# Scores of 256 instead of 512 keys a matmul, another order of the gelu's operations and a shorter warm-up in a two-layer decode kernel

## The chip, the cores and the metric

The kernel runs on one core of a Trainium2 chip. The metric is the device time of one execution in microseconds; what is compared is the median of several executions. A profiled execution also has a span, from the first to the last instruction in its trace, and the mean clock that TensorE (PE) was granted, as a share of full speed. In the profile PE is TensorE's matmuls, PEld its weight loads, DVE VectorE, ACT ScalarE, POOL GpSimd, and SP the engine whose queue issues all the transfers.

## The reference

One token (a row of 640 numbers) goes through two identical layers, each an attention over a cache and a mixer with a small MLP. Both layers use the same weights and the same caches. Cut to what is computed:

```python
def attention(x, k_cache, v_cache, wq, wo):        # 32 heads of 192, the last 4096 cached positions
    q = (x @ wq) per head
    p = softmax(q . k * 192 ** -0.5)
    return (p . v) for all heads, joined, @ wo

def mixer(x, w1, w2, w3, w4):
    ...                                            # the part with w1 and w2 only shifts along the sequence
    h2 = gelu(layernorm(x1) @ w3) @ w4             # 1536 units
    return x1 + h2

x = x + attention(layernorm(x)); x = x + mixer(layernorm(x))     # layer 1
x = x + attention(layernorm(x)); x = x + mixer(layernorm(x))     # layer 2
```

With a sequence of one, the groups that are shifted by one or two places are all zero, so the kernel needs w3 and w4 alone.

## The kernel before

A layer has 32 heads in 8 groups of 4 (`GROUPS`, reversed in layer 1, which the code calls layer 0). A head's keys and its values are one block each of 128 x 6144 bf16 (1536 KB), loaded from HBM into one of 11 cells (`take`, `give`, a first-in first-out list). All transfers stand in one fixed list, `stream`, and are issued from SP in its order: the query weights, then keys and values alternating (the next group's keys beside this group's values), the output weights of each group, and at a layer's end w3 and w4. A load is issued when its cell's last reader is done. The engines run their instructions in the order in which the code emits them (`manual_schedule`).

Seven turned key blocks (heads 0 to 6, `NKEEP`) are kept from layer 1 for layer 2 in cells of their own, so towards the end of layer 1 fewer cells are left for the stream. The other heads are turned into one shared cell, `area`.

For each head: `transpose_quart` (L351 to L373) turns a quarter of the key block with a DVE transpose (L370), four for a block. `scores` (L414) multiplies with the head's query columns (`Qblk`, 128 x 16 weights) into PSUM, and the 16 columns of the four heads of a group add into the same rows. `next_scores` (L438) decides on the shape. With `n == 4`, each of four quarters of the keys has its own rows (0, 32, 64 and 96) and a matmul has 256 keys; with `n == 2`, two halves of the keys have two row bands, and a matmul has 512 keys. A head has 24 matmuls in the first form and 12 in the second. `wide` in `attention` puts the first four groups of layer 1 and the third to fifth of layer 2 in the second form.

In the first form the scores of the first two quarters (`S(h, 0)`) stand ahead of those of the other two (`S(h, 1)`), so they can run while DVE turns the second half; in the second form each pair of matmuls needs quarters of both halves of the block, and all scores come at `half == 1`.

`softmax_steps` turns a group's scores into probabilities: maximum over the keys (L457, DVE), two small transposing products (L462, L479, PE), the exponential (L485, ACT), a transpose (L492, DVE), the rearranging products (L503, PE). `pv` multiplies with the values (L549, PE; 16 matmuls a head) and ends with a DVE transpose of the result (L556), which `o_fold` (L562, PE) adds up. `out_proj` (L571) multiplies with the output weights.

The loop of a group emits, for each head: the value product of this group's head, then turning and scoring of a head of the next group, then `o_fold`. Where two neighbouring groups have different forms, the first head's scores of the next group come only after `spread_max`.

`mixer` multiplies with w3 (L835) in two halves of the units, applies the gelu to each half (L840 to L854; squares and exponential on ACT, the rest on DVE), and multiplies with w4 (L867). In layer 2 both weights are loaded in pieces, and part of them is still there from layer 1.

At the start `WARM` matmuls of 32 x 32 (L309) run on PE while the query weights are on their way.

Of the kernel before, what the change touches and what calls it, by code (L numbers as in the profile page):

```python
# [36 lines left out]
def kernel(  # L37
# [40 lines left out]
    WARM = 125  # L78
# [273 lines left out]
    area = [None]  # L352

    def transpose_quart(layer, h, q):

        if layer == 1 and h < NKEEP:
            return kept[h]
# [3 lines left out]
        if layer == 0 and h < NKEEP:  # L361
            if q == 0:
                kept[h] = take(("T", h))
            T = kept[h]
        else:
            if area[0] is None:
                area[0] = take(("area", layer))
            T = area[0]
        Tu = T[:, q * QUART:(q + 1) * QUART].bitcast(U32).rearrange("p (y j b) -> p j y b", y=NY, j=NJ4)
# [45 lines left out]

    def scores(h, T, parts, ST, hq):

        ng = NGK // ST.n
        Q = Qblk[:, h // QH % 2, hq * QHEAD:(hq + 1) * QHEAD].rearrange("p (f x) -> p f x", x=QW)
        T5 = T[:].rearrange("p (g f i t) -> p g f i t", f=NFB, g=NGK, i=P)  # L420
        for f in range(NFB):
            for t in range(2):
                n = 2 * f + t
                for i in parts:
                    r = ST.rows.start + 32 * i
                    nc.tensor.matmul(  # L426
                        ST.ps[r:r + QW, :].rearrange("p (g i) -> p g i", g=ng), lhsT=Q[:, n, :],
                        rhs=T5[:, i * ng:(i + 1) * ng, f, :, t],
                        start=(hq == 0 and n == 0), stop=(hq == QH - 1 and n == NCOL - 1))

# [7 lines left out]
    def next_scores(n):  # L438
        turn[0] += 1
        i = turn[0] % 2  # L440
        if n == NT:
            return SimpleNamespace(n=n, rows=slice(0, P), ps=ST_both[:, i * SW:(i + 1) * SW])
        return SimpleNamespace(n=n, rows=slice(i * P // 2, (i + 1) * P // 2), ps=ST_both)
# [5 lines left out]
    def softmax_steps(n, ST, sc):  # L449
        held = {}  # L450
        R, np_ = ST.rows, ST.n
        NR, W_ = R.stop - R.start, P * NGK // np_
        ST_ps = ST.ps[R, :]

        def part_max():
            pm = big.tile([P, 1], F32, name="pm")
            nc.vector.tensor_reduce(out=pm[R, :], in_=ST_ps, op=ALU.max, axis=AX.X)  # L457
            held["pm"] = pm

        def turn_max():  # L460
            pmT_ps = psm.tile([1, NR], F32, tag="psm")
            nc.tensor.transpose(pmT_ps[0:1, :], held["pm"][R, 0:1], ident[R, R])  # L462
            held["pmT"] = pmT_ps

        def full_max():
            ngm = big.tile([1, 2 * QH], F32, name="ngm")
            nc.vector.tensor_reduce(out=ngm[:], in_=held["pmT"][0:1, :].rearrange("o (q x m) -> o x q m", q=np_, m=NM),
                                    op=ALU.max, axis=AX.XY, negate=True)

            wide = o_bytes[0:1, W_:W_ + 2 * NR].bitcast(F32)  # L470
            nc.vector.tensor_scalar(  # L471
                out=wide.rearrange("o (q x m) -> o q x m", q=np_, m=NM),
                in0=ngm[:].unsqueeze(1).unsqueeze(3).broadcast_to([1, np_, 2 * QH, NM]),
# [3 lines left out]
        def spread_max():  # L477
            nb_ps = psm.tile([P, 1], F32, tag="psm")
            nc.tensor.matmul(nb_ps[R, :], lhsT=held["w"],  # L479
                             rhs=ones[0:1, 0:1], start=True, stop=True)  # L480
            nb_sb = big.tile([P, 1], F32, name="nb_sb")
            nc.scalar.copy(nb_sb[R, :], nb_ps[R, :])  # L482
            Pr = o_bytes[R, 0:W_]
            lpart = big.tile([P, 1], F32, name="lpart")
            nc.scalar.activation(out=Pr, in_=ST_ps, func=ACTF.Exp,  # L485
                                 bias=nb_sb[R, 0:1], scale=sc[R, 0:1], accum_out=lpart[R, 0:1])
            held["Pr"], held["l"] = Pr, lpart

        def turn_p():

            for i in reversed(range(0, W_, SW)):
                nc.vector.transpose(o_bytes[R, SW + i:2 * SW + i], o_bytes[R, i:SW + i])  # L492
            lh = big.tile([P, QH], F32, name="lh")
            nc.vector.tensor_scalar(out=lh[R, :], in0=hm[R, :], scalar1=held["l"][R, 0:1], scalar2=None, op0=ALU.mult)
            held["lh"] = lh

        def swap():
            ng = NGK // np_
            PT_ps = psm.tile([P, n, NJ4, NGK], F32, tag="psm")
            src = o_bytes[R, SW:SW + W_].rearrange("p (g j i) -> p i j g", g=ng, j=NJ4)  # L500
            for m in range(NM):
                for q in range(np_):
                    nc.tensor.matmul(PT_ps[32 * m:32 * (m + 1), :, :, ng * q:ng * (q + 1)],  # L503
                                     lhsT=Eq[R, R.start // 32 + q, :], rhs=src[:, m:QW:NM], start=True, stop=True)
# [417 lines left out]
```

## Time and profile before

| | |
|---|---|
| three runs | 536.26, 543.6, 535.41 us; median 536.26 |
| profiled execution | 536.26 us, span 534.5, mean granted PE clock 0.659 |
| busy in the span | PE 321.0 us (60%), PEld 177.2 (33%), DVE 287.4 (54%), ACT 42.4 (8%), POOL 2.7 (1%) |
| moved from HBM | 216.47 MB, 405 GB/s over the span |
| scores (L426) | 336 matmuls of 512 keys, 864 of 256 |
| key transposes (L370) | about 0.94 us a quarter, 3.5 to 3.7 us a block |

How to read the lines that follow. A line of the windows gives a stretch in us, its length, the busy time and the number of instructions of PE, PEld, DVE, ACT and POOL, the granted PE clock, the share of the 16 DMA engines that was busy, and GB/s. A line of the waits gives the engine and line that waited, what it waited for, the total in us, how often, and the longest. A line of the timeline gives start and duration in us, engine, line, operation, tile written <- tiles read, shapes and the number of instructions that it merges, and in brackets how long the engine had been idle and what ended it. A DMA line ends with the us from issue to landing. SPq stands for instructions of SP's queue.

### The profile page before, as it was taken

To read this page: it belongs to the slowest core of one execution; us is meant where nothing else is said; L and a number is where in the kernel's file an instruction comes from. 1 tells how busy PE (TensorE), PEld (TensorE's weight loads), DVE (VectorE), ACT (ScalarE), POOL (GpSimd) and SP (SyncE) were. 2 spreads that over 40 slices of the span, in tenths; PEclk is the share of its full clock that TensorE was granted. 3 is DMA by queue.
4 is the path that set the end of the run, shared out by engine and by line. 5 is a ranking of instruction groups with operands and counts; after the bars stand their busy time and mean duration, and the time that the engine had idled before them with its cause. 6 is when DMAs were issued, how large, how long until landed. Compare 5 with 4: busy or idle time off the path is not lost. (4 is left out here: it accounts for less than half of the span.)

```text
span 534.5 us, 9507 instructions
## 1 busy us (share of the span) xinstructions
PE 321.0 (60%) x4125; PEld 177.2 (33%) x4125; DVE 287.4 (54%) x561; ACT 42.4 (8%) x157; POOL 2.7 (1%) x12
## 2 busy tenths in 40 slices
PE   3155474755646666667755865656565655667766
PEld 3011231313224343334433632323222243434435
DVE  2055646455555576656723355555547476666732
ACT  1000000101001010101011111000010000101012
POOL 2000000000000000000000000000000000000000
PEclk9996667556675767655665677665666557676665
DMA  8999999999999999999999999999999999999992
GB/s 342 429 425 427 421 427 427 425 427 423 424 427 390 425 423 408 344 397 380 388 418 405 377 420 427 425 425 424 427 423 426 424 419 423 424 424 426 419 403 109
DMA packets 23949, 217.08 MB, mean 406 GB/s; under 512 B 2532, under 2 KB 3044, under 8 KB 8420
## 3 DMA queue, kind: packets, MB, share of 16 engines
q1 hardware_dynamic: 23908, 216.48, 97.7%
q8 instruction: 32, 0.52, 0.4%
q14 instruction: 9, 0.07, 0.0%
HBM read 216.47 MB, written 0.00 MB: 405 GB/s over the span
## 5 line engine op out<-in xcount | busy, mean ns | idle before, releaser
L426 PEld LDWEIGHTS <-Qblk 128*16 128x16 bf16 x1200 | 66.7, 111 | 195.5 <-issue 179.1
L556 DVE STREAM_TRANSPOSE o_sb<-O_ps 128x384 f32<-128x384 f32 x64 | 37.2, 582 | 138.7 <-PE O_ps L549 138.7
L426 PE MATMUL ST_ps<-cell_336,Qblk 128*16 128x256 bf16 (+1 forms) x408 | 72.9, 485 | 55.3 <-DVE cell_336 L370 52.5
L426 PE MATMUL ST_ps<-cell_3261,Qblk 128*16 128x256 bf16 (+1 forms) x456 | 71.2, 454 | 45.3 <-DVE cell_3261 L370 39.9
L549 PEld LDWEIGHTS <-PT 128*2 128x2 bf16 x1024 | 45.6, 101 | 26.4 <-issue 17.4
L563 ACT ACTIVATE oT<-oT_ps,rl 32x6 bf16<-32x6 f32 x64 | 16.5, 258 | 293.2 <-PE oT_ps L562 236.4
L492 DVE STREAM_TRANSPOSE o_sb<-o_sb 64x256 bf16<-64x256 bf16 (+1 forms) x23 | 10.2, 442 | 40.1 <-ACT o_sb L485 27.8
L562 PE MATMUL oT_ps<-o_sb,Lq 128*32 128x6 f32 x256 | 21.8, 194 | 15.1 <-DVE o_sb L556 14.5
L562 PEld LDWEIGHTS oT_ps<-o_sb,Lq 128*32 128x32 f32 x256 | 20.4, 142 | 31.2 <-issue 27.1
L387 PE MATMUL qT_ps<-xc,wq_sb 128*128 128x1 bf16 x480 | 15.8, 165 | 14.9 <-DMA wq_sb<-in_A_wq_dram 14.0
L387 PEld LDWEIGHTS <-wq_sb 128*128 128x128 bf16 x480 | 14.7, 104 | 18.3 <-DMA wq_sb<-in_A_wq_dram 15.1
L462 PE MATMUL pmT_ps<-ident,pm 128*1 128x128 f32 (+1 forms) x16 | 4.4, 273 | 19.0 <-DVE pm L457 19.0
L401 PE MATMUL Qrep_ps<-Xq,Lb 128*128 128x24 bf16 (+1 forms) x18 | 3.3, 181 | 18.9 <-DVE Xq L394 18.6
L394 DVE TENSOR_TENSOR Xq<-qT_ps,maskq 128x24 bf16<-128x24 f32 (+1 forms) x18 | 2.8, 154 | 20.5 <-PE qT_ps L387 20.5
L508 PE MATMUL l_ps<-lh,ones 128*128 128x4 f32 (+1 forms) x32 | 9.2, 356 | 5.1 <-ACT PT L506 5.1
L479 PE MATMUL nb_ps<-ones,o_sb 1*128 1x1 f32 (+1 forms) x32 | 7.2, 292 | 7.5 <-DVE o_sb L471 7.5
L503 PEld LDWEIGHTS <-Eq 128*32 128x32 bf16 (+1 forms) x200 | 4.1, 111 | 21.0 <-issue 10.6
L479 PEld LDWEIGHTS nb_ps<-ones,o_sb 1*128 1x128 f32 (+1 forms) x32 | 6.0, 241 | 14.7 <-issue 12.0
L508 PEld LDWEIGHTS l_ps<-lh,ones 128*128 128x128 f32 (+1 forms) x32 | 7.8, 301 | 8.4 <-ACT PT L506 8.1
L485 ACT ACTIVATE o_sb<-ST_ps,nb_sb,sc 128x256 bf16<-128x256 f32 (+1 forms) x16 | 10.5, 656 | 0.5
L482 ACT COPY nb_sb<-nb_ps 128x1 f32<-128x1 f32 (+1 forms) x16 | 2.5, 157 | 94.1 <-PE nb_ps L479 94.1
L503 PE MATMUL PT_ps<-o_sb,Eq 128*32 128x32 bf16 (+1 forms) x200 | 7.0, 251 | 4.9 <-DVE o_sb L492 4.6
(291 smaller groups left out, 475.6 us busy)
## 6 DMA issues: line engine op xcount, KB each, us to landing
wq_sb<-in_A_wq_dram SPq DMA_DIRECT2D x5, 1536.0 KB, 14.3
cell_334<-in_A_k_cache_dram SPq DMA_DIRECT2D x1, 1536.0 KB
cell_356<-in_A_k_cache_dram SPq DMA_DIRECT2D x1, 1536.0 KB, 26.6
cell_381<-in_A_k_cache_dram SPq DMA_DIRECT2D x1, 1536.0 KB, 27.2
cell_399<-in_A_k_cache_dram SPq DMA_DIRECT2D x1, 1536.0 KB
cell_453<-in_A_k_cache_dram SPq DMA_DIRECT2D x1, 1536.0 KB, 29.5
cell_519<-in_A_v_cache_dram SPq DMA_DIRECT2D x1, 1536.0 KB, 29.5
cell_521<-in_A_k_cache_dram SPq DMA_DIRECT2D x1, 1536.0 KB, 29.5
```

The lines of the kernel that those rows point to most:

```text
L387: nc.tensor.matmul(qT_ps[:, tl:tl + 1], lhsT=wq_sb[:, kc, t * P:(t + 1) * P], rhs=xc[:, kc:kc + 1], start=(kc == 0), stop=(kc == ND - 1))
L426: nc.tensor.matmul(ST.ps[r:r + QW, :].rearrange("p (g i) -> p g i", g=ng), lhsT=Q[:, n, :], rhs=T5[:, i * ng:(i + 1) * ng, f, :, t], start ...
L462: nc.tensor.transpose(pmT_ps[0:1, :], held["pm"][R, 0:1], ident[R, R])
L479: nc.tensor.matmul(nb_ps[R, :], lhsT=held["w"], rhs=ones[0:1, 0:1], start=True, stop=True)
L485: nc.scalar.activation(out=Pr, in_=ST_ps, func=ACTF.Exp, bias=nb_sb[R, 0:1], scale=sc[R, 0:1], accum_out=lpart[R, 0:1])
L492: nc.vector.transpose(o_bytes[R, SW + i:2 * SW + i], o_bytes[R, i:SW + i])
L503: nc.tensor.matmul(PT_ps[32 * m:32 * (m + 1), :, :, ng * q:ng * (q + 1)], lhsT=Eq[R, R.start // 32 + q, :], rhs=src[:, m:QW:NM], start=Tru ...
L508: nc.tensor.matmul(l_ps[:], lhsT=ones[R, :], rhs=held["lh"][R, :], start=True, stop=True)
L549: nc.tensor.matmul(O_ps[r:r + 2, :], lhsT=PT[:, hq, 2 * i:2 * i + 2], rhs=v_pair(V, h, 2 * i * Dh, 2 * Dh), start=(i < 4), stop=(i >= NB - 4))
L556: nc.vector.transpose(o_sb[:], O_ps.rearrange("p (e a c) -> p e c a", e=2, c=NA))
L562: nc.tensor.matmul(oT_ps[r, :], lhsT=Lq[:], rhs=o_sb[:, e, :, e], start=(e == 0), stop=(e == 1))
L563: nc.scalar.activation(oT[r, :], oT_ps[r, :], ACTF.Copy, scale=rl[r, 0:1])
```

## The change

Four edits at once. The form with 512 keys a matmul goes, with all that chose between the two (`wide`, `parts`, `n`, `rows`); every group scores 256 keys a matmul. The shared cell of turned keys is handed out by quarters, in the order of their turning; the cells, the loads and DVE's order of transposes stay as they are. The gelu of a half, `h * r / (1 + e)`, was computed as the reciprocal of `(1 + e) * (1 / (h * r))` and becomes `(h * r)` times the reciprocal of `(1 + e)`. And the warm-up has 29 matmuls instead of 125.

```diff
-    WARM = 125
+    WARM = 29
...
-    def scores(h, T, parts, ST, hq):
-
-        ng = NGK // ST.n
+    def scores(h, Ts, q0, ST_ps, hq):
+
+        ng = NGK // NT
...
-                for i in parts:
-                    r = ST.rows.start + 32 * i
+                for i, T4 in enumerate(views):
+                    r = 32 * (q0 + i)
                     nc.tensor.matmul(
-                        ST.ps[r:r + QW, :].rearrange("p (g i) -> p g i", g=ng), lhsT=Q[:, n, :],
-                        rhs=T5[:, i * ng:(i + 1) * ng, f, :, t],
+                        ST_ps[r:r + QW, :].rearrange("p (g i) -> p g i", g=ng), lhsT=Q[:, n, :],
+                        rhs=T4[:, :, f, :, t],
                         start=(hq == 0 and n == 0), stop=(hq == QH - 1 and n == NCOL - 1))
...
-    def next_scores(n):
+    def next_scores():
         turn[0] += 1
         i = turn[0] % 2
-        if n == NT:
-            return SimpleNamespace(n=n, rows=slice(0, P), ps=ST_both[:, i * SW:(i + 1) * SW])
-        return SimpleNamespace(n=n, rows=slice(i * P // 2, (i + 1) * P // 2), ps=ST_both)
+        return ST_both[:, i * SW:(i + 1) * SW]
...
-        def S(h, half, ST, hq):
-            if ST.n == NT and (layer == 0 or h >= NKEEP):
-                parts = 2 * half, 2 * half + 1
-            elif half == 1:
-                parts = range(ST.n)
-            else:
+        def S(h, half, ST_ps, hq):
+            if layer == 1 and h < NKEEP:
+                if half == 1:
+                    scores(h, [Th.pop((h, q)) for q in range(NT)], 0, ST_ps, hq)
+                    give(("T", h))
                 return
-            scores(h, Th[h], parts, ST, hq)
...
+            scores(h, [Th.pop((h, q)) for q in (2 * half, 2 * half + 1)], 2 * half, ST_ps, hq)
...
-        wide = range(2, 5) if layer == 1 else range(4)
-        parts = [NT // 2 if gi in wide else NT for gi in range(len(groups))]
...
                     T(h0, 0)
                     part_max()
                     T(h0, 1)
-                    if ST.n == ST_n.n:
-                        S(h0, 0, ST_n, 0)
+                    S(h0, 0, ST_n, 0)
                     turn_max()
                     full_max()
-                    if ST.n == ST_n.n:
-                        S(h0, 1, ST_n, 0)
+                    S(h0, 1, ST_n, 0)
                     spread_max()
-                    if ST.n != ST_n.n:
-                        S(h0, 0, ST_n, 0)
-                        S(h0, 1, ST_n, 0)
...
             nc.scalar.activation(ge[:], gu[:], ACTF.Exp, scale=rg[:, 0:1])
-
-            rh = sm.tile([P, HF], F32, name="rh")
-            nc.vector.tensor_scalar(out=rh[:], in0=hp, scalar1=rr[:, 0:1], scalar2=None, op0=ALU.mult)
-            nc.vector.reciprocal(rh[:], rh[:])
-            nc.vector.scalar_tensor_tensor(out=gu[:], in0=ge[:], scalar=1.0, in1=rh[:],
-                                           op0=ALU.add, op1=ALU.mult)
-            with nc.allow_low_precision(reason="the matmul's operand, bf16 as in the reference"):
-                nc.vector.reciprocal(hT[:, half * HF:(half + 1) * HF], gu[:])
+            nc.vector.tensor_scalar(out=gu[:], in0=ge[:], scalar1=1.0, scalar2=None, op0=ALU.add)
+            nc.vector.reciprocal(gu[:], gu[:])
+            nc.vector.scalar_tensor_tensor(out=hT[:, half * HF:(half + 1) * HF], in0=hp, scalar=rr[:, 0:1], in1=gu[:],
+                                           op0=ALU.mult, op1=ALU.mult)
```

## The prediction, made before the result was known

> **What bounds the kernel now.** I read the page's totals first, then the stages by windows, the waits, one loop of each kind, and the end.
>
> ```profile
> span 534.5 us, 9507 instructions
> q1 hardware_dynamic: 23908, 216.48, 97.7%
> ```
>
> The queue is busy for 97.7% of the span, so at first sight the transfers bound the kernel and PE and DVE (60% and 54%) do not. The stages, with the rate in the last column, say where that fails:
>
> ```profile
> 10.00:160.00 150.00, 76.49 (x689) 32.56 (x689) 74.59 (x122) 7.41 (x26) 0.00 (x0) 0.71 1.01 425
> ...
> 160.00:170.00 10.00, 6.44 (x118) 4.50 (x119) 6.92 (x18) 1.29 (x4) 0.00 (x0) 0.50 0.96 380
> ...
> 200.00:270.00 70.00, 47.76 (x614) 28.59 (x602) 45.13 (x74) 5.21 (x20) 0.00 (x0) 0.63 0.98 384
> ...
> 290.00:310.00 20.00, 15.86 (x392) 12.51 (x391) 7.78 (x40) 3.02 (x15) 0.00 (x0) 0.67 0.99 383
> ```
>
> 425 GB/s is what the queue gives when it is full. From 160 to 170, 200 to 270 and 290 to 310 us it gives about 10% less: there are too few free cells, so loads are issued late. Who holds the cells? The two longest waits of DVE, and of PE, between 40 and 270 us (total, times, longest):
>
> ```profile
> DVE o_sb L556 <- PE O_ps L549: 63.5, 27, 4.3
> DVE o_sb L492 <- ACT o_sb L485: 12.8, 4, 3.8
> ...
> PE ST_ps L426 <- DVE cell_336 L370: 44.5, 35, 2.6
> PE Qrep_ps L401 <- DVE Xq L394: 11.6, 6, 3.2
> ```
>
> Neither engine waits for a transfer in that stretch. PE waits for DVE's key transposes, and DVE for PE's value products, which stand behind the scores: a ring, PE to DVE to PE, sets the pace, and the loads run ahead of it. How far ahead, for one key block in layer 1:
>
> ```profile
> L370 DVE STREAM_TRANSPOSE cell_336<-cell_1230 x4: 928/936/951, 157.2 to 160.4; 128x768 uint32<-128x768 uint32 x4
> L131 SPq DMA_DIRECT2D cell_1230<-in_A_k_cache_dram x1: 327/327/327, 127.3 to 127.3; - x1
> DMA to landing us min/median/max: 10.5/10.5/10.5
> ```
>
> It landed at 127.3 + 10.5 = 137.8 us and was first read at 157.2, 19.4 us later. The same view gives 9.5 us for the last key block of layer 2 (issued 475.3, landed after 17.4, read at 502.2). So the ring is late, and the transfers suffer only through the cells that it holds.
>
> **The change part by part.**
>
> *Scores.* Seven of the sixteen groups go from 512 to 256 keys a matmul: 28 heads, each with 24 matmuls instead of 12. What a group of four heads takes, by windows from the first value product of one group to that of the next, 512 keys first (the first, second and fourth lines), 256 keys in the others:
>
> ```profile
> 69.40:103.20 33.80, 20.15 (x204) 9.12 (x202) 18.59 (x33) 2.32 (x8) 0.00 (x0) 0.65 1.01 424
> 103.20:137.40 34.20, 20.35 (x204) 9.10 (x202) 19.00 (x33) 2.32 (x8) 0.00 (x0) 0.60 1.01 425
> 170.00:199.25 29.25, 18.84 (x262) 11.43 (x260) 17.95 (x32) 2.11 (x8) 0.00 (x0) 0.68 1.01 426
> 372.60:406.80 34.20, 20.70 (x204) 9.17 (x202) 18.56 (x33) 2.32 (x8) 0.00 (x0) 0.60 1.01 425
> 439.70:469.00 29.30, 18.87 (x262) 11.49 (x260) 17.98 (x31) 2.11 (x8) 0.00 (x0) 0.67 1.01 424
> ```
>
> The loads of a group are eight blocks of 1536 KB and one of 960 KB: 8 x 3.70 + 2.31 = 31.9 us at 425 GB/s. With 512 keys the ring (34.2) is slower than the transfers and falls behind by some 2 us a group; with 256 keys (29.3) it is faster and catches up 2.6 us. The reason is in one head of each kind:
>
> ```profile
> 76.48 2.72 PE L426 MATMUL ST_ps<-cell_336,Qblk 128*16 128x512 bf16 x11 [1.13 <-DVE cell_336 L370]
> ...
> 183.82 1.44 PE L426 MATMUL ST_ps<-cell_336,Qblk 128*16 128x256 bf16 x11 [0.58 <-DVE cell_336 L370]
> ```
>
> With 512 keys eleven of twelve matmuls stand behind the last transpose; with 256 keys half of them are done under the transposes. Of PE's work 2.72 - 1.44 = 1.3 us a head leaves the ring; the vector maximum, the exponential and the probability transposes of a group also shrink (0.67 to 0.40, 0.77 to 0.56, 0.91 to 0.45 us by the groups by line).
>
> What the ring gains: in layer 1 three loops (33.8 + 34.2 + 32.6 - 3 x 29.25 = 12.9 us), and the first group, whose keys are turned and scored from 27.4 to 53.3 us although the fourth block lands by 27.4 + 3 x 3.7 = 38.5: with 3.6 us of transposes and 1.5 of scores behind it, 43.6, so 9.7 us. Together 22.6 us. In layer 2 three loops, 34.6 + 34.2 + 32.9 - 3 x 29.3 = 13.8 us. This can't all be kept: the transfers take over as the bound. What is left is what they lose now.
>
> Term A, loads issued late in layer 1: 10 x (425 - 380) / 425 = 1.06 us and 70 x (425 - 384) / 425 = 6.75 us, together 7.8. A floor of 0 (the cells are short because seven turned key blocks are kept, whatever the pace) and a ceiling of 7.8; I take 7.8, since the ring comes at least 11 us (three transfers) earlier to each release between 200 and 250 us, while loads there are issued only two transfers ahead (8 to 10 us to landing). From the last value block of layer 1 (issued 275.2, landed 286.9, waited for by PE until 287.0) the serial part, with the dip at 290 to 310, follows as it is.
>
> Term B, the end. The last matmul weights:
>
> ```profile
> 511.29 2.22 SPq L176 DMA_DIRECT2D cell_5312<-in_B_w_dram  x2
> 526.78 0.40 PEld L835 LDWEIGHTS <-cell_5312 128*128 128x128 bf16 x12
> ...
> cell_5312<-in_B_w_dram SPq DMA_DIRECT2D x2, 768.0 KB, 10.7
> ```
>
> The second piece of w3 is issued at about 513.1 and lands 10.7 us later, 523.8. Behind it stand half of its 48 matmuls for the first half of the units, about 0.7 us, so 524.5 where the trace has 528.1: 3.6 us. The last piece of w4 lands at 517.5 + 9.9 = 527.4, with a few matmuls and the 2.9 us from 531.6 to the end behind it: 530.6 at the earliest, a gain of 3.9. The smaller counts: 3.6. The ring has to be 3.6 of 9.5 us earlier for it, and layer 2 gives it 13.8.
>
> *gelu.* Per half 5 DVE operations become 4, but two of the five (0.22 and 0.19 us) lie under the 0.30 us exponential, and behind it now stand three (add, reciprocal, product) instead of two. One step of 0.19 us more for each half: +0.4 us at the end; the same in layer 1 is covered by PE's 1.3 us wait there for w4. Bounds: -0.4 (two operations fewer, if DVE's queue counted) and +0.8. I take +0.4, by the exponential's row.
>
> *Warm-up.* 96 matmuls fewer of 125 (3.5 us, from 3.85 us). PE waits 14.0 us for the query weights behind them (the group of L387), so 0; if that cover were gone, at most 3.5 x 96/125 = 2.7 us won.
>
> *Order.* The loads, their cells and DVE's transposes keep their order, so SP's and POOL's queues see nothing moved. Of the 96 x 2 PE instructions gone and 28 x 24 + 112 added, none issues a transfer.
>
> Sum, against the profiled execution's 536.26 us (span 534.5 and 1.8 around it; it is also the median of the three runs): 536.26 - 7.8 - 3.6 + 0.4 = 525.3.
>
> *Rules weighed.* The Trainium skill, Perfetto Trace Analysis, "Optimizing Tensor Performance", says that larger matmuls are more efficient, which speaks against the change. In this trace that holds for PE alone: a head's 24 small ones cost it 2 x 1.57 us, the twelve large ones 2.97. By the rule, with all of 28 x 0.17 on the path, the time would be 541. The skill's TensorE: Matmul & The Clock Gate, Part 1, says that the array is slow until some 3.4 us of activity release it; fewer warm-up matmuls would then cost. Here pairs of 512-key matmuls take 0.43 us at 31 us (granted clock 1.00) and at 44.6 us (0.50) alike, so by either the sum stays.
>
> **The rivals.**
> 1. The forecast, both terms: 525.3, its own range 522.8 to 527.8.
> 2. More: the dip at 290 to 310 us goes too, 20 x (425 - 383) / 425 = 2.0: 523.3. For it: the ring is early there. Against it: those cells are freed by a serial part that still starts at the last value block.
> 3. Only the end: the kept blocks starve the queue at any pace, and of term A only the 1.06 stays: 536.3 - 1.1 - 3.6 + 0.4 = 532.0.
> 4. Only term A: layer 2's ring stays late at the end: 536.3 - 7.8 + 0.4 = 528.9. Against it: 34.2 to 29.3 a group.
> 5. No change: the queue at 97.7% is all there is, the ring's pace is lost elsewhere: 536. Against it: 7.8 us of dips and 9.5 us of lateness.
> 6. Slower: the additional PE instructions land in the ring. The place is the last half of each head's scores: twelve matmuls at p us each against 2.72. Rows give p = 1.44 / 11 = 0.13 at clock 0.50 and 0.07 (0.85 us for twelve, 189 us) at a higher one; it decides from p = 0.227. At p = 0.30 each head loses 0.9 us, 28 heads 25 us, 561. Only a clock far below every row would do that.
>
> **How the numbers follow.** Chances: 0.58, 0.11, 0.11, 0.07, 0.08 and 0.05, in this order. The likeliest is 525.3. 2% is about what a measurement of this kernel can tell from no change; that line is 525.5, inside the forecast's own range. Of the 0.58 I put 0.37 below it (small dips, such as 10 x (425 - 416) / 425 = 0.2 us at 430 to 440, are not in the sum), with rival 2 0.48; the other 0.21 and rivals 3, 4 and 5 make 0.47; slower 0.05. The range takes in rivals 3 and 4 and most of 2: 521.0 to 532.5, leaving rivals 5 and 6 and a little more.
>
> **What would show it.** In the changed profile the rate at 160 to 270 us should be 420 or more (term A; 384 would be rival 3), PE or DVE should wait for cells' transfers in layer 1 and 2 (now they do not), key blocks should be read within a few us of landing, and groups should take about 31.9 us instead of 29.3 or 34.2. At the end PE should wait for w3 or w4 (term B). DVE's three gelu operations should follow the exponential. Wrong would be: groups over 34 us in layer 1, matmuls of 256 keys slower than 0.2 us each, or a queue below 425 GB/s although loads stand in it.

## The result, and the profile after

The kernel after takes 527.95 us (median of four runs, 527.72 to 528.32) where the kernel before took 537.26 beside it (535.41 to 543.6). The ratio is 0.9839, with a 95% interval of 0.9805 to 0.9873; it compares the means without the run of 543.6, which was in a slower state of the chip. So the change is 1.6% quicker, clear of no change and short of 2%. The profiled execution took 527.87 us, 526.1 of them its span. All of what follows about single waits comes from this one execution.

The page after: the span, the load queue, and the shares of the chain that ended last.

```profile
span 526.1 us, 10080 instructions
...
q1 hardware_dynamic: 23908, 216.48, 98.5%
...
DMA 56%; PE 20%; DVE 18%; issue 4%; ACT 1%; SPq 1%; DVEq 0%; ACTq 0%
```

The same bytes move, in 8.4 us less. The third line says that transfers are on the chain that ended last for 56% of the span. The line of the kernel before (PE 4%, DVE 2%) can't be set beside it as it stands: there the chain could be followed back only to 499.7 us, the last 35 us. Over these 35 us it names PE and DVE and no transfer; over the last 35 us of the kernel after, the chain is two transfers until 518.7 us, and the tail of the mixer.

The stretches in which the queue had given 380, 384, 417 and 383 GB/s before:

```profile
160.00:170.00 10.00, 4.87 (x48) 2.56 (x48) 4.14 (x5) 0.51 (x2) 0.00 (x0) 0.58 1.01 426
200.00:270.00 70.00, 41.51 (x560) 25.31 (x561) 39.08 (x71) 5.81 (x22) 0.00 (x0) 0.66 1.01 422
270.00:290.00 20.00, 11.36 (x206) 7.42 (x205) 7.14 (x28) 2.97 (x13) 0.00 (x0) 0.50 1.00 395
290.00:310.00 20.00, 14.07 (x315) 9.89 (x315) 7.93 (x28) 1.84 (x8) 0.00 (x0) 0.76 0.96 381
```

The first two dips are gone. The last one stays, and 270 to 290 us has become one. By the prediction's own formula the queue now loses 20 x (425 - 395) / 425 + 20 x (425 - 381) / 425 = 3.5 us from 270 to 310 us, where it lost 2.4 before.

The waits from 40 to 270 us (total, times, longest):

```profile
DVE o_sb L549 <- PE O_ps L542: 54.9, 28, 2.8
PE ST_ps L426 <- DVE cell_240 L370: 31.9, 36, 3.4
...
DVE cell_240 L370 <- DMA cell_1672<-in_A_k_cache_dram: 2.8, 1, 2.8
...
DVE cell_240 L370 <- DMA cell_1347<-in_A_k_cache_dram: 2.4, 1, 2.4
```

DVE now waits for key blocks to land, in a stretch where it had never done so. The view of one tile says how near. It is the load with the same place in the stream as the one shown before, which had landed at 137.8 us and been read 19.4 us later:

```profile
L370 DVE STREAM_TRANSPOSE cell_240<-cell_1347 x4: 935/946/978, 137.5 to 140.4; 128x768 uint32<-128x768 uint32 x4
L130 SPq DMA_DIRECT2D cell_1347<-in_A_k_cache_dram x1: 328/328/328, 109.5 to 109.5; - x1
...
DMA to landing us min/median/max: 27.8/27.8/27.8
```

It is issued 17.8 us earlier, lands at 109.5 + 27.8 = 137.3, and is read at once. The landing is where it was, because the queue was full in both kernels up to there; only the reader has come forward. The last key block of layer 2, 9.5 us late before, lands at 459.6 + 28.1 = 487.7 and is read at 487.8.

The first four groups of layer 1, from one value product to the next, all with 256 keys:

```profile
57.45:86.59 29.14, 19.27 (x261) 11.84 (x260) 18.00 (x32) 2.11 (x8) 0.00 (x0) 0.62 1.01 424
86.59:116.39 29.80, 18.78 (x259) 11.72 (x258) 18.26 (x32) 2.11 (x8) 0.00 (x0) 0.67 1.01 425
116.39:148.23 31.84, 19.53 (x259) 11.80 (x258) 18.24 (x32) 2.11 (x8) 0.00 (x0) 0.66 1.01 424
148.23:181.53 33.30, 19.13 (x261) 11.83 (x260) 18.39 (x32) 2.11 (x8) 0.00 (x0) 0.60 1.01 424
```

This is catching up as it looks in a profile: 29 us a group as long as landed blocks lie in the cells, then 32 to 33, about the pace of the loads (31.9).

One product of PE in layer 1's mixer, and two at the end:

```profile
291.10 0.42 PE L845 MATMUL y_ps<-hT,wx_sb 128*128 128x1 bf16 x10 [1.07 <-DMA wx_sb<-in_B_w_dram]
...
513.69 0.56 PE L564 MATMUL y_ps<-oT,cell_5560 128*128 128x1 bf16 x15 [0.65 <-DMA cell_5560<-in_A_wo_dram]
...
518.79 0.48 PE L817 MATMUL V_ps<-xc,cell_5597 128*128 128x1 bf16 x12 [0.95 <-DMA cell_5597<-in_B_w_dram]
```

At the end PE waits for output weights and then for w3's second piece. In layer 1 it waits for w4's last piece, which it had not done before (the line of the kernel before stands below, with the gelu's term). And the new gelu, the three operations behind the exponential of the first half:

```profile
520.19 0.17 DVE L829 TENSOR_SCALAR gu<-ge 128x6 f32<-128x6 f32 x1 [0.37 <-ACT ge L828]
520.39 0.19 DVE L830 RECIPROCAL gu<-gu 128x6 f32<-128x6 f32 x1
520.62 0.22 DVE L831 SCALAR_TENSOR_TENSOR hT<-V_ps,r,gu 128x6 bf16<-128x6 f32 x1
```

From the square of the first half to the end of the second half's last operation it is 519.36 to 521.93, 2.57 us; before it was 528.16 to 530.36, 2.20. In layer 1's mixer the same stretch also takes 2.57 us (286.73 to 289.30) where it took 2.21.

### The profile page after: what moved, and what is told of

The parts are those of the page before. It is cut to its first block, busy times and chain, and to the rows that moved or that the text cites. A ratio compares the mean times of both kernels' runs of the same rounds, so it can differ in the third digit from the quotient of the medians.

```text
span 526.1 us, 10080 instructions
## 1 busy us (share of the span) xinstructions
PE 316.7 (60%) x4421; PEld 194.6 (37%) x4421; DVE 283.8 (54%) x550; ACT 40.9 (8%) x157; POOL 2.7 (1%) x12
## 4 chain that ended last, share of the span: by engine, by line
DMA 56%; PE 20%; DVE 18%; issue 4%; ACT 1%; SPq 1%; DVEq 0%; ACTq 0%
PE ST_ps L426 8%; DVE cell_240 L370 6%; PE O_ps L542 6%; DVE cell_3381 L370 6%; DMA cell_5020<-in_A_v_cache_dram 6%; DMA cell_1672<-in_A_k_cache_dram 6%; DMA cell_5276<-in_A_k_cache_dram 5%; DMA cell_1347<-in_A_k_cache_dram 5%; DMA cell_1997<-in_A_k_cache_dram 5%; DMA cell_4714<-in_A_k_cache_dram 5%; DMA cell_1022<-in_A_k_cache_dram 5%; DMA cell_5498<-in_A_v_cache_dram 5%; DMA cell_238<-in_A_k_cache_dram 4%; DMA kx<-in_A_v_cache_dram 2%; DMA cell_2559<-in_A_v_cache_dram 2%
## 5 line engine op out<-in xcount | busy, mean ns | idle before, releaser
L426 PEld LDWEIGHTS <-Qblk 128*16 128x16 bf16 x1536 | 86.1, 111 | 188.2 <-issue 162.8
L426 PE MATMUL ST_ps<-cell_240,Qblk 128*16 128x256 bf16 x600 | 68.8, 384 | 56.4 <-DVE cell_240 L370 40.7
L426 PE MATMUL ST_ps<-cell_3381,Qblk 128*16 128x256 bf16 x600 | 68.1, 383 | 44.9 <-DVE cell_3381 L370 31.3
L485 DVE STREAM_TRANSPOSE o_sb<-o_sb 128x256 bf16<-128x256 bf16 x16 | 7.1, 445 | 33.7 <-PE qT_ps L387 20.5
L496 PEld LDWEIGHTS <-Eq 128*32 128x32 bf16 x256 | 4.9, 114 | 24.7 <-issue 24.6
L501 PE MATMUL l_ps<-lh,ones 128*128 128x4 f32 x32 | 9.0, 352 | 5.4 <-ACT PT L499 5.4
L501 PEld LDWEIGHTS l_ps<-lh,ones 128*128 128x128 f32 x32 | 7.6, 295 | 8.0 <-ACT PT L499 7.7
L474 PEld LDWEIGHTS nb_ps<-ones,o_sb 1*128 1x128 f32 x32 | 7.4, 285 | 7.4 <-issue 5.5
L496 PE MATMUL PT_ps<-o_sb,Eq 128*32 128x32 bf16 x256 | 7.2, 236 | 4.6 <-DVE o_sb L485 4.6
L474 PE MATMUL nb_ps<-ones,o_sb 1*128 1x1 f32 x32 | 8.7, 338 | 1.5 <-DVE o_sb L466 1.5
L480 ACT ACTIVATE o_sb<-ST_ps,nb_sb,sc 128x256 bf16<-128x256 f32 x16 | 9.0, 564 | 0.5
L426 PE MATMUL ST_ps<-cell_2327,Qblk 128*16 128x256 bf16 x48 | 4.4, 410 | 5.4 <-DVE pm L451 5.1
```

Source lines behind the costliest of these rows:

```text
L426: nc.tensor.matmul(ST_ps[r:r + QW, :].rearrange("p (g i) -> p g i", g=ng), lhsT=Q[:, n, :], rhs=T4[:, :, f, :, t], start=(hq == 0 and n == ...
L474: nc.tensor.matmul(nb_ps[:], lhsT=held["w"], rhs=ones[0:1, 0:1], start=True, stop=True)
L480: nc.scalar.activation(out=Pr, in_=ST_ps, func=ACTF.Exp, bias=nb_sb[:, 0:1], scale=sc[:, 0:1], accum_out=lpart[:, 0:1])
L485: nc.vector.transpose(held["PrT"], held["Pr"])
L501: nc.tensor.matmul(l_ps[:], lhsT=ones[:], rhs=held["lh"][:], start=True, stop=True)
```

## The experiments

A ratio is a kernel's time over that of the kernel before, run on the same chip in the same rounds. The kernel before has medians of 536.6 to 537.7 us there, so kernels that did not run side by side are compared by their ratios, or by one instruction's place in the traces. `e1` to `e4` ran side by side, and so did `e5` to `e7` on another chip, and `after_again` with `e8` to `e10` on the first chip again; `e11` ran on a third.

### One edit at a time

`e1`: the kernel after with the old gelu and the old warm-up, so the scoring alone.

```diff
-    WARM = 29
+    WARM = 125
...
-            nc.vector.tensor_scalar(out=gu[:], in0=ge[:], scalar1=1.0, scalar2=None, op0=ALU.add)
-            nc.vector.reciprocal(gu[:], gu[:])
...
+            nc.vector.tensor_scalar(out=rh[:], in0=hp, scalar1=rr[:, 0:1], scalar2=None, op0=ALU.mult)
+            nc.vector.reciprocal(rh[:], rh[:])
...
+                nc.vector.reciprocal(hT[:, half * HF:(half + 1) * HF], gu[:])
```

> The kernel after with the old gelu (five VectorE operations for a half) and the old warm-up of 125 matmuls: only the scoring in quarters is left of the change. My theory (the scoring carries the gain through the ring of the two stages; the new gelu's operations cost 0.37 us in the last tail): 527.5 us, that is 0.3 to 0.5 us below the kernel after, and 9 to 10 us below the kernel before; the four rows behind the last exponential take 2.2 us instead of 2.57. Rival (the gelu with one operation less is itself a part of the gain): 0.5 us or more above the kernel after, 528.5 to 529.

Measured: 526.9 us, ratio 0.9789 (0.9741 to 0.9836). The kernel after's own ratio, 0.9839, is not parted from it: the whole gain is there, and the forecast difference of 0.4 us is too small to see. The rows behind the exponential take 2.21 us, as expected.

`e2`: the kernel before with the new gelu (the gelu lines of the diff above, the other way round).

> The kernel before with the new gelu alone. My theory: the kernel before plus 0.3 to 0.5 us (about 536.7 beside 536.3), since three operations follow the exponential where two did, and in layer 1 the mixer's half is covered by TensorE's wait for w4's last piece. Rival (one operation less is time less on a chain that VectorE holds): 0.3 us or more below the kernel before.

Measured: 538.78 us, ratio 1.0017 (0.9982 to 1.0052). The sign is the expected one, the interval holds no change. But layer 1's mixer doesn't cover the new gelu: from the product with the last value block to the product with w4's last piece it is 9.88 us (286.62 to 296.50), and 9.51 in the kernel before (287.00 to 296.51). So the 0.37 us are paid in each layer.

`e3`: the kernel before with the short warm-up.

```diff
-    WARM = 125
+    WARM = 29
```

> The kernel before with 29 warm-up matmuls in place of 125 and nothing else. My theory: no change (within 0.3 us of the kernel before), because the first key block's landing starts the work, and the granted clock over the first 40 us is the same. Rival (the warm-up decides the clock of the first stages): 2 us or more slower, with a lower granted clock in the first 60 us. Rival (warm-up matmuls stand in front of the first projections): up to 2.7 us faster.

Measured: 536.05 us, ratio 0.9971 (0.9937 to 1.0006). The scoring carries the change; the other two edits are below what the intervals tell from zero. But `e3`'s trace shows something that no theory had: the first weights come earlier. PE's wait for the second piece of them, first before, then in `e3`:

```profile
12.67 0.18 PE L387 MATMUL qT_ps<-xc,wq_sb 128*128 128x1 bf16 x1 [3.49 <-DMA wq_sb<-in_A_wq_dram]
```

```profile
10.70 0.18 PE L387 MATMUL qT_ps<-xc,wq_sb 128*128 128x1 bf16 x1 [1.58 <-DMA wq_sb<-in_A_wq_dram]
```

And the transfers of the first 15 us of the kernel before, by queue (packets, MB, share of 16 engines):

```profile
q1 hardware_dynamic: 487, 5.29, 88.3%
q8 instruction: 1, 0.02, 0.4%
```

A block of instructions (16 KB, 0.97 us in the packets of the trace, at 9.4 us) runs among the weights' packets; the profile counts both as work of the same 16 engines. With 29 warm-up matmuls no such block runs in that stretch. All six kernels with 101 or 125 warm-up matmuls have the block, at 9.2 to 9.8 us, and start that product at 12.04 to 12.67; all eight with 29 have none and start it at 10.69 to 11.20. So the longer warm-up costs 0.8 to 2.0 us of landing there; that the block is the way it does so is read from this company, and was not tried by itself.

### One layer at a time

`e4` and `e5`: the kernel before with 256 keys in one layer only, layer 1 in `e4` (the diff), layer 2 in `e5` (`range(0) if layer == 1 else range(4)`).

```diff
-        wide = range(2, 5) if layer == 1 else range(4)
+        wide = range(2, 5) if layer == 1 else range(0)
```

> The kernel before with 256 keys a matmul in all of layer 1, and 512 keys kept in the three middle groups of layer 2 (old gelu, old warm-up). My theory (the two terms are separate, and the ring's lateness in layer 1 is what made the queue run dry): the rate at 200 to 270 us goes to about 422 GB/s, the last value block of layer 1 is read about 7 us earlier, the mixer of layer 1 gives 1.5 to 2 us of it back, and the end is 5 us below the kernel before: 531 us. Rival (the two layers' lateness adds up, so that the last stage is late whichever one is mended): 535 us. Rival (layer 1 alone carries all of it): 528 us.

> The kernel before with 256 keys a matmul in all of layer 2, and 512 keys kept in the first four groups of layer 1 (old gelu, old warm-up). My theory: layer 1 is as before (rate of 364 to 390 GB/s at 200 to 270 us), the last piece of w4 is issued as late as before but the end no longer hangs on the ring, and the time is 3.5 to 3.8 us below the kernel before: 532.6 us. Rival (the end follows the ring of layer 1): no change.

Measured: `e4` 530.82 us, ratio 0.9865 (0.9819 to 0.9911); `e5` 533.17, ratio 0.9924 (0.9896 to 0.9952). The product of the two ratios, 0.979, is that of `e1`: the two parts add up. It also settles a part of the change that no run takes by itself: `e4` and `e5` still hand out the shared cell of turned keys whole, so handing it out by quarters is not what brings the gain. Windows of `e4`, then of `e5`:

```profile
200.00:270.00 70.00, 42.99 (x564) 26.00 (x568) 39.01 (x71) 5.82 (x22) 0.00 (x0) 0.65 1.01 422
```

```profile
200.00:270.00 70.00, 47.65 (x608) 28.60 (x601) 45.19 (x74) 5.26 (x20) 0.00 (x0) 0.63 0.98 384
```

Layer 1's shape alone fills or empties the queue there. In `e5` the last load of w4 is issued only 0.46 us earlier than before, and yet the span ends 4.2 us earlier, with PE waiting for the weights as in the kernel after:

```profile
518.24 0.56 PE L571 MATMUL y_ps<-oT,cell 128*128 128x1 bf16 x15 [0.66 <-DMA cell<-in_A_wo_dram]
...
523.36 0.48 PE L835 MATMUL V_ps<-xc,cell 128*128 128x1 bf16 x12 [0.96 <-DMA cell<-in_B_w_dram]
```

So the end was the ring of layer 2, and is the transfers now.

### Why 256 keys are quicker

`e7` takes away what the prediction gave as the reason: all scores of a head are emitted behind its last key transpose. (Three of the 24 still start earlier, each when its own quarter is turned.)

```diff
-            scores(h, [Th.pop((h, q)) for q in (2 * half, 2 * half + 1)], 2 * half, ST_ps, hq)
+            if half == 0:
+                return
+            scores(h, [Th.pop((h, q)) for q in range(NT)], 0, ST_ps, hq)
```

> The kernel after with all 24 score matmuls of a head behind its last key transpose, in place of half of them under the transposes of the second half. Theory (the ring has some us to spare at 256 keys, with half of the matmuls under the transposes): the ring of a group is longer by 4 x 0.4 to 0.7 us, 31 to 32 us for a group beside 31.9 us of loads, and the time is 0 to 2 us above the kernel after. Rival (what carries the gain is the overlap of scores and transposes, and not the shape of the matmul): 4 us or more above the kernel after, with the wide groups' 33.8 us back.

Measured: 526.95 us, ratio 0.9814 (0.978 to 0.9849), no slower than the kernel after. One head in `e7`, then one at the same place of the kernel after:

```profile
195.63 0.37 PE L426 MATMUL ST_ps<-cell,Qblk 128*16 128x256 bf16 x1 [0.49 <-DVE cell L370]
196.49 1.44 PE L426 MATMUL ST_ps<-cell,Qblk 128*16 128x256 bf16 x21 [0.49 <-DVE cell L370]
```

```profile
194.96 1.23 PE L426 MATMUL ST_ps<-cell_240,Qblk 128*16 128x256 bf16 x12 [0.59 <-DVE cell_240 L370]
196.68 1.44 PE L426 MATMUL ST_ps<-cell_240,Qblk 128*16 128x256 bf16 x11 [0.49 <-DVE cell_240 L370]
```

Behind the last transpose stand 21 matmuls in the one and 11 in the other, and both take 1.44 us. The 21 fill four bands of 32 output rows; the 11 fill two, the matmuls of the other two bands having run under the transposes. The 11 wide ones that took 2.72 us before also fill two, with twice the columns. The ring is as quick in `e7`: its first groups take 29.1 and 28.7 us from one value product to the next. So the overlap of scores and transposes is there in the kernel after, but the gain doesn't need it if bands run at the same time. `e8` tests that reading: the bands one after the other.

```diff
-        for f in range(NFB):
-            for t in range(2):
-                n = 2 * f + t
-                for i, T4 in enumerate(views):
+        for i, T4 in enumerate(views):
+            for f in range(NFB):
+                for t in range(2):
+                    n = 2 * f + t
```

> The kernel after once more, unchanged, as the measure for the other three on the same chip: 526 to 528.5 us. The seven profiles so far say that one program's executions differ by about 2 us once the transfers are the bound (524.4 to 526.6 us of span in e6).

> The kernel after with the scores' loops turned round: all six matmuls of a quarter (one band of 32 output rows) one after the other, then the next quarter, in place of one of each band in turn. Theory (matmuls whose outputs lie in different row bands run at the same time, four of them in the narrow form and two in the wide one, and that is what made 2.72 us of eleven wide matmuls and 1.44 us of twenty-one narrow ones): a matmul of 256 keys in a band of its own costs 0.21 us at the halved clock, 0.11 at the full one; a head whose keys are all turned already (the seven kept ones in layer 2) takes 2.6 to 5.1 us for its 24 matmuls where it takes 0.7 to 1.4 now, the start of layer 2 is longer by 8 to 15 us, and the time is 5 to 15 us above the kernel after. In the ring little changes, since only the last quarter's six (about 1.3 us) stand behind the last transpose. Rival (a matmul costs its columns, in whatever rows): no change, within 1 us.

Measured: `after_again` 526.99 us, ratio 0.9806 (0.9778 to 0.9834); `e8` 528.46, ratio 0.9837 (0.9812 to 0.9862). In `e8`, the end of one head in the ring, and a head of layer 2 whose keys were kept; then such a head in `after_again`:

```profile
197.10 0.42 PE L426 MATMUL ST_ps<-cell,Qblk 128*16 128x256 bf16 x1
...
197.31 0.41 PE L426 MATMUL ST_ps<-cell,Qblk 128*16 128x256 bf16 x1
...
197.52 0.41 PE L426 MATMUL ST_ps<-cell,Qblk 128*16 128x256 bf16 x1
...
298.58 1.56 PE L426 MATMUL ST_ps<-cell,Qblk 128*16 128x256 bf16 x24
```

```profile
298.65 0.86 PE L426 MATMUL ST_ps<-cell,Qblk 128*16 128x256 bf16 x24
```

Within one band a matmul starts 0.21 us after the one ahead of it (at a granted clock of 0.50), as expected. How the first matmuls of the two kept heads start, at the full clock, is in short windows of this line alone, where the first bracket counts PE's matmuls, first in `after_again`, then in `e8`:

```profile
298.60:298.67 0.07, 0.02 (x4) 0.02 (x6) 1.00 1.64 702
298.60:298.76 0.16, 0.11 (x4) 0.11 (x8) 1.00 1.44 614
298.60:298.79 0.19, 0.14 (x8) 0.12 (x12) 1.00 1.21 517
```

```profile
298.50:298.68 0.18, 0.10 (x1) 0.10 (x2) 1.00 0.64 273
```

In `after_again` four start within 10 ns of each other (298.653 to 298.663), one in each band, and the next four 0.11 us later. In `e8` the first (at 298.585) is alone for 0.11 us. So the bands do run at once. The cost of losing it was overrated: 1.5 us instead of 5 to 15, which is also more than the rival's 1 us, so it is the starts that decide and not the time. A kept head takes 1.56 us and not the 2.6 of 24 matmuls at 0.11 us each, so the bands still overlap in part. And the clock that PE was granted went up; how much of the small cost is owed to that, no run parts. From 310 to 400 us, `e8`, then `after_again`:

```profile
310.00:400.00 90.00, 63.53 (x844) 38.81 (x834) 57.30 (x102) 7.10 (x27) 0.00 (x0) 0.81 1.01 425
```

```profile
310.00:400.00 90.00, 60.92 (x814) 36.38 (x814) 54.82 (x96) 6.84 (x26) 0.00 (x0) 0.61 1.01 425
```

In the ring the three orders come to the same. The last transpose of the head shown ends at 196.63 us in the kernel after, 196.44 in `e7` and 196.44 in `e8`, and its scores end at 198.12, 197.93 and 197.94: 1.5 us later in each, all at a clock of 0.50. What stands behind that transpose is a row of about six matmuls of 256 keys in each of two bands, in each of four, or in one (in `e8` the other quarters ran under the transposes). In the kernel before it was a row of about six of 512 keys in each of two bands, and 2.8 us (76.42 to 79.20). So scores that run under the transposes (the kernel after, `e8`) and four bands side by side (`e7`) are each enough; no run takes both away.

### Lateness, and the best version

`e9` is the kernel before with the short warm-up and one wide group, the second of layer 1:

```diff
-    WARM = 125
+    WARM = 29
...
-        wide = range(2, 5) if layer == 1 else range(4)
+        wide = range(0) if layer == 1 else range(1, 2)
```

`e10` has no wide group: it is `e1` with `WARM = 29`, the kernel after with the old gelu.

> Only the second group of layer 1 scores 512 keys a matmul; everything else 256 (old gelu, warm-up of 29). Theory (lateness is caught up: a wide group falls 2 us behind the transfers, a narrow one wins back 2.6, and what counts is whether the ring is late when cells run short at the end of the layer): 0 to 0.7 us above the kernel of e10. Rival (each wide group costs its share of the 7 us in layer 1): 1.8 us or more above it.

> The kernel after with the old gelu: 256 keys a matmul and the short warm-up stay. Theory (the new gelu costs 0.37 us in the last tail and nothing else): 0.2 to 0.5 us below the kernel after, the lowest time of all. Rival (the two gelus are alike to the end, or the mixer of layer 1 decides): no difference that the executions' scatter lets one see, or the kernel after ahead.

Measured: `e9` 525.75 us, ratio 0.9786 (0.9761 to 0.9811); `e10` 525.88, ratio 0.9792 (0.9767 to 0.9817). One wide group costs nothing (0 to 0.7 us above `e10` was expected, 0.1 below was measured): the loop in which it is scored takes 33.1 us and the next two 28.4 and 29.3, so it falls behind and they catch up. Both are ahead of the kernel after beside them (526.99) and have the lowest times of the study, though by its ratio `e1` (0.9789) is level with them. That the gelu does all of it in `e10` is not shown: 1.1 us is more than the 0.37 of the tail, and the executions overlap (525.74 to 526.52 and 526.18 to 527.70).

### Where layer 1's gain leaks

In the kernel after, layer 1's last value block is read 7.1 us earlier than before (279.87, not 287.00), but layer 2's first key block is issued only 5.66 us earlier: w4's last piece lands 11.9 us after its issue instead of 10.5. `e6` was to part two causes: it moves the giving back of w3's cell from behind the product with w3 to behind that with w4.

```diff
-        give(("w3", layer))
...
+        give(("w3", layer))
```

> The kernel after with one step moved: the cell of w3 is given back behind the product with w4 instead of ahead of it, so that the first value block of layer 2 in that cell is issued some 3.5 us later in layer 1's mixer. Theory one (the last piece of w4 in layer 1 lands 11.9 us after its issue because that value block shares the transfer engines with it): TensorE's wait of 1.07 us for the piece at 290 us falls to under 0.4 us, the mixer ends up to 1 us earlier, and the time is between 0.7 us less and 1 us more than the kernel after, as the value block's lateness decides. Theory two (the piece is last in engines that were out of step long before): the piece lands as late, the wait stays at 0.9 us or more, and the time is 0 to 2 us above the kernel after.

Measured: 527.53 us, ratio 0.9814 (0.9782 to 0.9845). It told nothing of the two: the value block is issued at 286.55 us, where the kernel after issues it (286.50). The order in which cells are given back did not set that load. Its six spans, 524.4 to 526.6 us, do show how far the executions of one such program lie apart.

`e9`'s trace answered the first theory without meaning to. It issues that value block at 286.58 too, and w4's last piece lands 10.5 us after its issue. So sharing the engines with the value block is not by itself what delays it. A second suspect was another block of instructions, 9.6 us behind the issue in the kernel after and in `e10`, and 6.8 us behind it in `e9`. `e11` moves it by PE's instructions alone, on `e10`:

```diff
-    WARM = 29
+    WARM = 101
```

> The kernel of e10 with 101 warm-up matmuls in place of 29, and nothing else. The traces so far show blocks of 16 KB of instructions loaded through the same 16 transfer engines, each holding one engine for about 1.1 us; in e10 and in the kernel after one of them runs 9.6 us after the last piece of w4 of layer 1 was issued, just ahead of its landing. The 72 more matmuls put PE's instructions where they stand in e9 (e9 has 112 fewer, and 112 + 2 x 72 is one block of 256). Theory (the block of instructions delays one engine's share of w4's last piece): the block runs some 7 us after the issue as in e9, the piece lands 10.4 to 10.5 us after its issue instead of 12.0, TensorE's wait of 1.53 us for it goes, the first key block of layer 2 is issued 7.0 us earlier than in the kernel before instead of 5.7, and the time is 0 to 1 us below e10. Rival (which engine straggles is settled by the order of the transfers, and the blocks have nothing to do with it): landing after 11.8 to 12.0 us and a wait of 0.9 us or more, as in e10.

Measured: 526.95 us, ratio 0.98 (0.9762 to 0.9838). The block moved to 4.3 us behind the issue, and the piece still took 11.8 us. In `e10`, then in `e11`, then in `e9`:

```profile
291.07 0.42 PE L848 MATMUL y_ps<-hT,wx_sb 128*128 128x1 bf16 x10 [1.53 <-DMA wx_sb<-in_B_w_dram]
```

```profile
289.09 1.36 PE L848 MATMUL y_ps<-hT,cell 128*128 128x1 bf16 x45 [2.40 <-DMA cell<-in_B_w_dram]
290.31 0.27 PE L848 MATMUL y_ps<-hT,wx_sb 128*128 128x1 bf16 x5
290.80 0.43 PE L848 MATMUL y_ps<-hT,wx_sb 128*128 128x1 bf16 x10 [0.22 <-DMA wx_sb<-in_B_w_dram]
```

```profile
289.46 0.68 PE L867 MATMUL y_ps<-hT,wx_sb 128*128 128x1 bf16 x15
```

The wait moved to the piece ahead and did not go. `e7` says the same from the other side: its block runs 9.6 us behind the issue, as in the kernel after, and its piece lands after 10.5. The second suspect falls as well. How much earlier than in the kernel before each load is issued, in us (the second column is a landing, the last a span), for the kernels with all groups, or all but one, at 256 keys:

| | w4's last piece, layer 1 | its landing after the issue | layer 2's first key block | layer 2's last load | span |
|---|---|---|---|---|---|
| before | 0 | 10.5 | 0 | 0 | 534.5 |
| after | 7.12 | 11.9 | 5.66 | 5.01 | 526.1 |
| after_again | 7.18 | 11.8 | 5.91 | 5.13 | 525.9 |
| e6 | 7.09 | 12.0 | 5.59 | 6.61 | 524.6 |
| e8 | 7.19 | 11.8 | 4.72 | 4.34 | 526.8 |
| e10 | 7.25 | 12.0 | 5.70 | 6.22 | 524.6 |
| e11 | 7.24 | 11.8 | 5.96 | 6.11 | 524.7 |
| e1 | 6.31 | 10.9 | 5.89 | 5.85 | 524.9 |
| e7 | 6.77 | 10.5 | 6.55 | 6.70 | 524.5 |
| e9 | 7.08 | 10.5 | 7.05 | 8.19 | 524.1 |

A late piece comes with 1.2 to 1.6 us lost there (more in `e8`, whose kept heads take longer), a punctual one with 0 to 0.2. `e1` lies between, and has lost 1.3 us one step earlier: its last value block is read at 281.22 us, not at 279.87 (in `e4` at 281.08). `e6` is the kernel after in all but the step that did nothing, and its 6.61 beside 5.01 says that the last column differs by 1.6 us between executions of the same loads. Most of w4 passes at the same time in both kinds (the median of its packets of 2560 bytes starts at 284.8 to 285.0 us in `after`, `after_again`, `e10` and `e9`), and the last of them end at 290.3 to 290.6 us in the first three and at 289.2 in `e9`. What makes them late stays open.

## Why the prediction was right, and where it was not

- **What bounds the kernel.** Right. The ring was late against the transfers, and the loads suffered through the cells: with the lateness gone, the load shown is issued 17.8 us earlier, and the queue is full at 160 to 170 and 200 to 270 us.
- **The reason in one head.** The size was right (2.72 to 1.44 us), and so is "with 256 keys half of them are done under the transposes" as a description: twelve run there, eleven stand behind the last transpose. But it is not what the gain hangs on, since `e7` all but takes that overlap away and has the same 1.44 us. What counts is how many columns the fullest band still has to take behind the last transpose, and with quarters in four bands that is the same in either order. The Trainium skill has the ground for it (TensorE: Matmul & The Clock Gate, Part 3, "Packing small matmuls — row/col tiling"): small matmuls whose outputs start at different multiples of 32 rows run concurrently in the array. The trace agrees, with four starts within 10 ns. The rule of larger matmuls, which the prediction weighed, didn't hold here: where both forms fill two bands a head's matmuls cost PE about the same (2 x 1.57 and 2.97 us), and four narrow bands at once (`e7`) take about half as long as two wide ones (1.44 and 2.72).
- **Term A, 7.8 us.** This is the step that was mis-sized. The dips went as it said, and 7.1 us arrived at layer 1's last value block. "The serial part ... follows as it is" then failed: 1.5 us were lost at w4's last piece and 0.65 more up to the last load, so 5.0 arrived. `e7` and `e9` kept 6.7 and 8.2 of it, and `e6`, with the kernel after's loads, 6.6: a part of what is missing is the scatter of single executions.
- **Term B, 3.6 us, and gelu, +0.4.** Together 3.2 net; measured 8.4 - 5.0 = 3.4 net, and 0.37 of gelu in the tail. Which weights would count was right too (w3's second piece, 0.95 us); that the output weights ahead of them also make PE wait (0.65 us) was not foreseen. `e5`, with the old gelu, has term B alone: 4.2 - 0.46 = 3.7. For layer 1 the prediction misread a wait. PE's 1.3 us there were for the gelu and not for w4, as the first line says (before); the second is from the kernel after:

```profile
295.22 1.43 PE L867 MATMUL y_ps<-hT,cell_2820 128*128 128x1 bf16 x45 [1.30 <-DVE gu L843]
```

```profile
288.27 1.63 PE L845 MATMUL y_ps<-hT,cell_2940 128*128 128x1 bf16 x45 [1.47 <-DVE hT L831]
```

  So nothing covered the new gelu in layer 1, and `e2` pays 0.37 us there. In the kernel after the late piece of w4 covered it (1.07 us of wait left), which no one had foreseen: that +0.4 fits is luck in this part.
- **Sum.** 536.26 - 5.0 - 3.4 = 527.9, the profiled execution, at the upper edge of the forecast's own range (527.8) and well inside the whole one. The 2.6 us between it and 525.3 are term A's in that execution. Run again the kernel came closer: 525.3 would be a ratio of 0.980, the first measurement gave 0.9839 (from 0.9805), `after_again` 0.9806 (0.9778 to 0.9834).
- **Warm-up, 0.** Costed by the wrong cover. PE's wait for the query weights hides the matmuls, but with the longer warm-up those weights land 0.8 to 2.0 us later. `e3`'s span is 1.1 us shorter than the one before, which is within what single executions scatter. Where the transfers are the bound there is no sign of it: `e1`, with 125, is as quick as the rest. That the clock would not care held: no slowdown in `e3`. The clock of 1.00 that the prediction read at 31 us is doubtful, though: its pairs of 512 keys take 0.43 us there as at 0.50, while matmuls of 256 keys start 0.11 us apart in a band where the clock is 1.00 at 298 us, so 512 would take about 0.22 (an estimate).
- **Rivals.** The second didn't come (381 GB/s at 290 to 310 us, as before). The third and fourth are refuted by `e4` and `e5`: each term is there without the other. The fifth and sixth are out by the result.

## What to carry to other kernels

When a queue is busy for 97% and dips by 10% in places, look at how long a landed block waits for its reader: here 19 us, with neither PE nor DVE waiting for a transfer, meant that compute was late and cells were the link. A gain taken from such a ring ends where the transfers take over, so size it by what the queue lost and not by what the ring wins, and count every serial part behind it as a place where some of it leaks. For thin matmuls, count the columns that the fullest band of 32 output rows still has to take at the moment that matters, before counting instructions.

## What the runs showed of the hardware

- At the half clock a 256-column matmul starts 0.21 us after the one ahead of it in its own band of 32 output rows, and 11 in two bands take as long (1.44 us) as 21 in four. At the full clock four in four bands start within 10 ns of each other, and the next four 0.11 us later.
- The granted clock of the kernel that ran the bands one after the other was 0.769 on the mean and 0.81 from 310 to 400 us, against 0.643 and 0.61 with the bands side by side, at the same work and the same rate of loads. PE was busy for 63.5 and 60.9 of those 90 us. What made the difference in clock was not tested.
- Blocks of 16 KB of instructions run among the packets of the 16 transfer engines, about 1 us each (0.97 in the kernel before), and 72 more warm-up matmuls moved one from 9.6 to 4.3 us behind an issue (`e10`, `e11`); at the start of the program the six kernels that load one ahead of 10 us got their second piece of weights 0.8 to 2.0 us later than the eight that don't.
- The last piece of a run of loads landed 10.5 us after its issue in five kernels (`before`, `e2`, `e5`, `e7`, `e9`), 10.9 in `e1` and `e4`, 11.6 in `e3`, and 11.8 to 12.0 in six, alike in `after` and `after_again` (11.9 and 11.8). The cause stays open.
